# A store moved from GpSimd's DMA queue to ScalarE's, and half of a weight piece asked for two units later, in an mLSTM cell with a SwiGLU block

## The chip, the cores and the metric

The kernel runs on one core of one Trainium2 chip. Its time is device microseconds of one execution; the figure compared is the median of several runs. A core has TensorE (PE), VectorE (DVE), ScalarE (ACT), GpSimd (POOL) and SyncE (SP), each with an instruction stream of its own that it works through in order, and 16 DMA engines that all queues share. SyncE, ScalarE and GpSimd can ask for DMA transfers.

## The reference, cut to what matters

```
# q, k, v, o_gate: (4, 8, 768, 40); i_gate, f_gate: (4, 8, 768); all float32
m = -1e30; C = 0; n = 0
for t in range(768):
    m_new  = max(f_gate[t] + m, i_gate[t])
    f_stab = exp(f_gate[t] + m - m_new); i_stab = exp(i_gate[t] - m_new); m = m_new
    C = f_stab * C + i_stab * outer(v[t], k[t]);  n = f_stab * n + i_stab * k[t]
    y[t] = sigmoid(o_gate[t]) * (C @ q[t]) / max(|n . q[t]|, 1)
x = y as (3072, 320)                      # tokens x (heads * head_dim)
out = (silu(x @ w_gate) * (x @ w_val)) @ w_out     # d_ff = 1536; the weights are float64
```

## The kernel before, in words

The 768 steps are cut into six chunks of 128 tokens. For a chunk the cell is computed in matrix form: scores of q and k, weighted by exponentials of differences of the gates' running sums and running maxima, plus what a state carried from chunk to chunk gives. Each chunk's 512 tokens (four batches) then go through the SwiGLU block. The cell of the next chunk is worked in between the matmuls of the block of the present one. The whole order is written out by hand: every engine gets its instructions in the order of the program text, and semaphores make it wait where data demands it.

The change lies in the block of chunk 0, at some 30 to 95 us. The block's first half runs in twelve units, `hidden(0, m)` for m = 0 to 11 (L741): ten matmuls (20 records in the profile) of x against 128 gate and 128 value columns into two PSUM banks (L749), a SiLU on ScalarE into `tmp` (L754), and a multiply on VectorE into `h_sb` (L755). Behind each unit stand the steps of its slot (`slots`, L1013). They prepare chunk 1: loads, the late gates, transposes, weights.

Meanwhile the weights arrive. They are float64 and are read as pairs of 32-bit words in pieces (`PIECES`, L163). Piece 8 holds blocks 10 and 11, that is gate and value columns of units 10 and 11. `piece_load` (L167) asks for a piece in three parts: part 0, the gate half, on SyncE (640 KB); parts 1 and 2, the value half, on GpSimd (512 and 128 KB). A block is turned into float32 just ahead of use by `convert` (L254): two scalings on ScalarE (`scale`, L227 and L229), a join on VectorE (L236, L237) and an addition (L244) on GpSimd, or for blocks 9 to 11 on VectorE. `ahead` (L1012) says which block is converted inside which unit: block 8 in unit 6, block 9 in unit 7, block 10 in unit 8, block 11 in unit 9. The conversion stands ahead of the unit's SiLU in ScalarE's stream.

The weights of the cell need the running maxima of all later steps in another layout. `late_maxima` (L331) computes them on VectorE into `M_sb`, `M_store` (L343) writes them to `M_dram` in 320 rows of 256 bytes, and `weights_load` (L513) reads them back, spread over partitions, into `w_sb` (two loads of 512 KB). That load is asked for on SyncE and waits for the store's completion. Behind it in SyncE's stream stand the loads of q and v of chunk 1 (`load`, L138), which write rows of 160 bytes, and the gate half of piece 8. `weights_cap` (L529), `weights_sub` (L518) and `weights_exp` (L537) work on `w_sb`. `turn_one` (L347) transposes k in slot 6, and q in the middle of unit 8 (`amid`, L1029); ScalarE copies the results to `kT` and `qT`. The scores (L385) come in slot 8.

The loads and stores asked for by SyncE and ScalarE take eight completion semaphores in turn, those of GpSimd eight others; a transfer waits for the one eight places before it.

Of the kernel before, what the change touches and what calls it, by code (L numbers as in the profile page):

```python
# [13 lines left out]
AF = mybir.ActivationFunctionType  # L14
# [10 lines left out]
def kernel(  # L25
# [18 lines left out]
    nc = tc.nc  # L44
# [63 lines left out]
    k_sb = const.tile([128, BH, DP], F32)  # L108
    q_sb = const.tile([128, BH, DP], F32)
    v_sb = const.tile([128, BH, D1], F32)  # L110
# [3 lines left out]
    kT = const.tile([128, PP, L], F32)  # L114
# [197 lines left out]
    step1 = keep1  # L312
# [250 lines left out]
    A, V, G = nc.scalar, nc.vector, nc.gpsimd  # L563
# [82 lines left out]
    GATE, VALUE = (0,), (1, 2)  # L646
# [357 lines left out]
    def load_all(dst, a, n, eng=nc.sync):  # L1004
# [3 lines left out]
    run = lambda f, *a, **b: (lambda: f(*a, **b))  # L1008
# [4 lines left out]
    slots = {  # L1013
        0: [run(piece_load, 6), run(piece_load, 7, wo_sb)],
        1: [run(late_sums)],
        2: [run(late_maxima), run(M_store, G), run(load_all, k_sb, k, 1)],
        3: [run(late_decay), run(weights_load, 1), run(load_all, q_sb, q, 1), run(load_all, v_sb, v, 1)],
        4: [run(nc.scalar.activation, step1, step1, AF.Exp), run(decay_rows), run(cap_table), run(piece_load, 8)],
        5: [run(late_turns), run(decay)],
        6: [run(turn_one, P, k_sb, kT, (A, A)) for P in range(2)] + [run(weights_cap, 0), run(weights_cap, 1), run(piece_load, 9)],  # L1020
        7: [run(weights_sub, 1, 0), run(weights_sub, 1, 1), run(weights_exp, 0), run(weights_exp, 1), run(weigh_values, G, 0),
            run(weigh_values, G, 1)],
        8: [run(nc.gpsimd.memset, q_sb, 0.0), run(do_scores), run(piece_load, 10), run(load_all, o_sb, o_gate, 1)],
# [128 lines left out]
```

## Time and profile before

| | |
|---|---|
| Time, median of 3 runs | 516.13 us (515.53 to 517.15) |
| Profiled execution: time / span of its instructions | 516.18 us / 514.3 us |
| Mean granted TensorE clock | 0.997 |
| Busy: TensorE, its weight loads | 504.4 us (98%), 425.7 us (83%) |
| Busy: VectorE, ScalarE, GpSimd | 333.0 us (65%), 208.3 us (40%), 264.0 us (51%) |
| Moved by DMA | 43.31 MB in 184187 packets, 173080 of them under 512 B |
| DMA queues, share of 16 engines | SyncE's 45.5%, GpSimd's 4.7% |

A line of a timeline reads: start and length in us, engine, line of the kernel, operation, output <- input, shapes, count, and in brackets how long the engine stood idle before it and what released it. "SPq" is SyncE's queue issuing transfers; such a line lasts as long as the issue, not the transfer. A store or load runs some microseconds on after its issue. Times of single packets and of completions come from the DMA records of the same trace. TensorE's ends are modelled, so a stretch in which it runs at half clock looks busy as well.

### The profile page before, as it was taken

What the parts mean: (1) busy time and instruction counts of PE and PEld (TensorE: products, weight loads), DVE (VectorE), ACT (ScalarE), POOL (GpSimd) and SP (SyncE); (2) the same over time, 40 slices, a digit from 0 to 9 for tenths busy, and PEclk for the clock granted to TensorE, in tenths of its full rate; (3) what the DMA queues carried; (4) which work ended last, traced back from release to release, by engine and by line L of the source; (5) the groups of instructions that cost most, each with busy time, mean ns of one, the idle gap of its engine ahead of it and who ended that gap; (6) DMA issues with size and microseconds to landing.
All of it is one profiled execution on the core that took longest, in us unless ns stands there. A gap on an engine that the chain in (4) does not pass through costs nothing.

```text
span 514.3 us, 15103 instructions
## 1 busy us (share of the span) xinstructions
PE 504.4 (98%) x6437; PEld 425.7 (83%) x6437; DVE 333.0 (65%) x543; ACT 208.3 (40%) x404; POOL 264.0 (51%) x296
## 2 busy tenths in 40 slices
PE   8999989999899999999999999999999999999997
PEld 4854545677788899888899988899988899988897
DVE  5889658697798778578468578558558554233421
ACT  3674846439333339321338321347431330123210
POOL 3674432365689672357652447651447750166710
PEclk9999989999999999999999999999999999999999
DMA  9999997799611992501992411992100200100001
GB/s 147 180 211 229 182 172 213 162 157 108 108 29 26 162 129 39 90 6 25 163 133 35 83 13 20 163 132 40 41 3 16 39 3 20 33 1 0 1 14 40
DMA packets 184187, 43.31 MB, mean 84 GB/s; under 512 B 173080, under 2 KB 179624, under 8 KB 183480
## 3 DMA queue, kind: packets, MB, share of 16 engines
q1 hardware_dynamic: 182308, 36.95, 45.5%
q0 software_dynamic: 1680, 5.33, 4.7%
q8 instruction: 51, 0.84, 0.7%
q14 instruction: 16, 0.13, 0.1%
q10 hardware_dynamic: 132, 0.07, 0.0%
HBM read 35.68 MB, written 4.01 MB: 77 GB/s over the span
## 4 chain that ended last, share of the span: by engine, by line
PE 83%; DMA 7%; ACT 4%; POOL 2%; DVE 1%; SPq 1%; issue 1%; ACTq 0%; POOLq 0%; DVEq 0%
PE gv_x L899 24%; PE o_ps L820 22%; PE gv_y L899 20%; PE gv_ps L749 3%; DMA q_sb<-in_q_dram 3%; PE o_ps L766 3%; DMA raw<-in_moe_w_val_dram 3%; PE inter L434 2%; PE intra L443 2%; PE sp L385 2%; ACT w_sb L535 2%; DMA h_sb<-in_moe_w_val_dram 1%; PE add L411 1%; SPq L369 1%; ACT h_sb L584 1%
## 5 line engine op out<-in xcount | busy, mean ns | idle before, releaser
L899 PE MATMUL gv_x<-xT,wgv_sb 64*128 64x256 f32 x720 | 89.3, 377 | 0.0
L899 PEld LDWEIGHTS gv_x<-xT,wgv_sb 64*128 64x128 f32 x720 | 69.7, 187 | 7.9 <-issue 0.2
L820 PE MATMUL o_ps<-wo_sb,h_sb 128*128 128x160 f32 x480 | 67.4, 300 | 0.0
L820 PEld LDWEIGHTS o_ps<-wo_sb,h_sb 128*128 128x128 f32 x480 | 65.6, 190 | 1.7 <-issue 1.7
L947 ACT ACTIVATE h_sb<-gv_x 128x256 f32<-128x256 f32 x30 | 11.5, 385 | 115.7 <-PE gv_x L899 115.7
L749 PE MATMUL gv_ps<-xT,wgv_sb 64*128 64x512 f32 x240 | 56.2, 612 | 0.1
L749 PEld LDWEIGHTS gv_ps<-xT,wgv_sb 64*128 64x128 f32 x240 | 25.6, 190 | 24.8 <-issue 20.7
L899 PE MATMUL gv_y<-xT,wgv_sb 64*128 64x256 f32 x360 | 44.0, 376 | 0.0
L899 PE MATMUL gv_y<-q_sb,wgv_sb 64*128 64x256 f32 x360 | 44.0, 376 | 0.0
L396 POOL TENSOR_TENSOR vw_sb<-v_sb,w_sb 128x656 f32<-128x656 f32 x10 | 14.0, 1400 | 53.2 <-ACT w_sb L535 40.1
L899 PEld LDWEIGHTS gv_y<-q_sb,wgv_sb 64*128 64x128 f32 x360 | 35.1, 187 | 3.9
L899 PEld LDWEIGHTS gv_y<-xT,wgv_sb 64*128 64x128 f32 x360 | 35.1, 187 | 3.9
L820 PE MATMUL o_ps<-wT,S 128*128 128x160 f32 x240 | 33.4, 299 | 0.0
L820 PEld LDWEIGHTS o_ps<-wT,S 128*128 128x128 f32 x240 | 32.9, 190 | 0.0
L899 PE MATMUL gv_x<-q_sb,sw 64*128 64x256 f32 x240 | 31.1, 377 | 1.4 <-POOL sw L873 1.4
L535 ACT ACTIVATE w_sb<-w_sb,g_T 128x64 f32<-128x64 f32 x128 | 31.0, 335 | 0.0
L920 POOL TENSOR_TENSOR h_sb<-x_sb 128x512 f32<-128x512 f32 x12 | 15.7, 1306 | 24.6 <-ACT x_sb L919 24.6
L940 POOL TENSOR_TENSOR tmp<-tmp 128x512 f32<-128x512 f32 x15 | 20.1, 1342 | 15.0 <-DVE tmp L939 15.0
L920 POOL TENSOR_TENSOR h_sb<-tmp 128x512 f32<-128x512 f32 x13 | 16.5, 1272 | 21.5 <-ACT tmp L919 21.5
L787 POOL TENSOR_TENSOR S<-h_sb 128x256 f32<-128x256 f32 x30 | 22.7, 756 | 9.3 <-DVE h_sb L920 7.3
L899 PE MATMUL gv_y<-q_sb,sw 64*128 64x256 f32 x200 | 27.1, 389 | 0.2 <-DVE tmp L917 0.2
L766 PE MATMUL o_ps<-wo_sb,h_sb 128*128 128x320 f32 x96 | 27.2, 438 | 0.0
(226 smaller groups left out, 988.9 us busy)
## 6 DMA issues: line engine op xcount, KB each, us to landing
w_sb<-M_dram SPq DMA_DIRECT2D x10, 512.0 KB
v_sb<-in_v_dram SPq DMA_DIRECT2D x12, 320.0 KB
o_sb<-in_o_gate_dram SPq DMA_DIRECT2D x12, 320.0 KB
raw<-in_moe_w_out_dram SPq DMA_DIRECT2D x3, 1280.0 KB
k_sb<-in_k_dram SPq DMA_DIRECT2D x10, 320.0 KB
x_sq<-k_sb SPq DMA_DIRECT2D x64, 40.0 KB
q_sb<-in_q_dram SPq DMA_DIRECT2D x32, 64.0 KB
out_dram<-tmp SPq DMA_DIRECT2D x24, 80.0 KB
```

What stands on the lines that cost most here:

```text
L385: nc.tensor.matmul(sp[two][half(i), a, :], lhsT=kT[feats(two), P * UA + a, half(i)], rhs=qT[feats(two), P * UA + a, half(i)], start=True, ...
L396: eng.tensor_tensor(vw_sb[:, heads(P)], v_sb[:, heads(P)], w_sb[:, heads(P), last].to_broadcast([128, UH, D1]), op=ALU.mult)
L434: nc.tensor.matmul(inter[two][half(i), a, :], lhsT=qT[feats(two), P * UA + a, half(i)], rhs=state(2 * n + i)[feats(two), P * UA + a, :], s ...
L535: nc.scalar.activation(w_sb[:, h], w_sb[:, h], AF.Exp, bias=g_T[:, n, h:h + 1], scale=-1.0)
L749: nc.tensor.matmul(ps[i], lhsT=wgv_sb[half(i), m, kc, :], rhs=x[half(i), kc, :], start=(kc == 0), stop=(kc == NKC - 1))
L766: nc.tensor.matmul(ps[u], lhsT=hid(g, m)[:, ts(u, L)], rhs=wo_sb[:, m, :], start=(m == 0), stop=(m == NFC - 1))
L787: eng.tensor_tensor(S1[:, k], lo[:, second_half], hi[:, second_half], op=ALU.add)
L820: nc.tensor.matmul(node[x][:, i], lhsT=lhs(k)[:, ts(i, L)], rhs=rhs(k), start=start and k == 0 and i == 0, stop=stop and k == KH - 1, skip ...
L899: nc.tensor.matmul(ps[:, i, cols], lhsT=lhs(c)[half(i)], rhs=rhs(c)[half(i)], start=start and c == 0, stop=stop and c == n - 1, skip_group ...
L920: (nc.vector if k == KH - 1 else nc.gpsimd).tensor_tensor(h_sb[:, 2 * k + 1], uw[:, 0], uw[:, 1], op=ALU.mult)
L940: nc.gpsimd.tensor_tensor(uw[:, :, second_half], uw[:, :, second_half], uw[:, :, first_half], op=ALU.add)
L947: nc.scalar.activation(h[:, first_half], x[:, 0, first_half], AF.Silu)
```

## The change

The store of the maxima is asked for by ScalarE, at the start of slot 3, where GpSimd asked for it in slot 2. In ScalarE's stream it comes behind the SiLU of unit 3 and ahead of the scalings of block 6; on the other side GpSimd's addition of block 6 no longer has it ahead. Piece 8's gate half stays in slot 4 on SyncE. Its value half moves from slot 4 to the start of slot 6: in GpSimd's stream it comes behind the additions of blocks 7 and 8, where it stood ahead of both. No arithmetic is added or removed. The store takes one of the semaphores that SyncE and ScalarE share, so each later transfer of theirs has the next one.

```diff
-        2: [run(late_maxima), run(M_store, G), run(load_all, k_sb, k, 1)],
-        3: [run(late_decay), run(weights_load, 1), run(load_all, q_sb, q, 1), run(load_all, v_sb, v, 1)],
-        4: [run(nc.scalar.activation, step1, step1, AF.Exp), run(decay_rows), run(cap_table), run(piece_load, 8)],
+        2: [run(late_maxima), run(load_all, k_sb, k, 1)],
+        3: [run(M_store, A), run(late_decay), run(weights_load, 1), run(load_all, q_sb, q, 1), run(load_all, v_sb, v, 1)],
+        4: [run(nc.scalar.activation, step1, step1, AF.Exp), run(decay_rows), run(cap_table), run(piece_load, 8, parts=GATE)],
         5: [run(late_turns), run(decay)],
-        6: [run(turn_one, P, k_sb, kT, (A, A)) for P in range(2)] + [run(weights_cap, 0), run(weights_cap, 1), run(piece_load, 9)],
+        6: [run(piece_load, 8, parts=VALUE)] + [run(turn_one, P, k_sb, kT, (A, A)) for P in range(2)] + [run(weights_cap, 0), run(weights_cap, 1), run(piece_load, 9)],
```

## The prediction

> **What bounds the kernel now.** I read the busy slices first: TensorE is busy for 504.4 us of 514.3, so only what TensorE loses counts. Next, all its waits over 0.15 us behind the first 22 us: 0.40 and 1.57 us at 68 to 70 us, 0.56 at 91.7, 0.37 at 96.2, 1.40 at 137.6, 0.17 at 142.2. The first two are the only ones a load causes, and both are for q of the second chunk (L139). Timeline of TensorE around them (start us, us, line, out<-in, count, wait):
>
> ```profile
> 60.70 7.09 PE L749 MATMUL gv_ps<-xT,wgv_sb 64*128 64x512 f32 x32
> 68.20 0.71 PE L352 MATMUL tp_kq<-x_sq,q_sb 64*128 64x64 f32 x16 [0.40 <-DMA q_sb<-in_q_dram]
> 70.48 0.71 PE L352 MATMUL tp_kq<-x_sq,q_sb 64*128 64x64 f32 x16 [1.57 <-DMA q_sb<-in_q_dram]
> 71.00 3.66 PE L749 MATMUL gv_ps<-xT,wgv_sb 64*128 64x512 f32 x8
> 74.59 2.09 PE L385 MATMUL sp<-qT,kT 40*64 40x64 f32 x128
> ```
>
> Eight matmul records take 3.66 us here, while 40 take 9.76 us later. The table by stretches says why (after each colon: length, busy time by engine, granted clock, DMA share, GB/s):
>
> ```profile
> 54.00:55.40 1.40, 1.40 (x16) 0.99 (x14) 1.26 (x2) 1.38 (x3) 1.26 (x4) 1.00 0.27 30
> 55.40:57.00 1.60, 1.60 (x8) 0.80 (x10) 0.38 (x2) 1.59 (x3) 1.48 (x2) 1.00 1.08 307
> 57.00:62.00 5.00, 5.00 (x52) 2.75 (x50) 3.01 (x7) 3.14 (x7) 1.78 (x2) 1.00 0.98 200
> 67.50:71.10 3.60, 1.63 (x36) 1.25 (x36) 3.53 (x4) 1.09 (x2) 0.00 (x0) 1.00 0.78 120
> 71.10:74.50 3.40, 3.40 (x11) 1.12 (x8) 0.00 (x0) 2.96 (x5) 1.48 (x2) 0.50 1.07 210
> ```
>
> The granted clock is 0.50 for the 3.4 us behind the waits and 1.00 elsewhere after the first microseconds. So this place costs 1.97 us of waiting and 1.7 us of half rate, together 3.7 us. The third thing to see: the DMA engines idle at 54.0 to 55.4.
>
> Why q is late stands in the timelines of SyncE's queue and of GpSimd:
>
> ```profile
> 32.77 18.07 SPq L139 DMA_DIRECT2D k_sb<-in_k_dram  x1
> 53.83 1.18 SPq L516 DMA_DIRECT2D w_sb<-M_dram  x2
> 55.10 8.78 SPq L139 DMA_DIRECT2D q_sb<-in_q_dram  x2
> ...
> 47.06 0.63 POOL L344 DMA_DIRECT2D M_dram<-M_sb  x1 [1.90 <-DVE M_sb L334]
> 54.38 1.17 POOL L202 DMA_DIRECT2D raw<-in_moe_w_val_dram  x2
> ```
>
> and in the list of waits of SyncE's queue (us in total, times, longest):
>
> ```profile
> SPq L516 <- DMA M_dram<-M_sb: 2.9, 1, 2.9
> ```
>
> SyncE is free at 50.84 but waits until 53.83 for the store of the maxima. The store's own packets run only at 51.7 to 53.1, behind the 4 KB packets of earlier value halves on GpSimd's queue. The value half of piece 8 then shares 57 to 62.8 us with the w_sb loads, ahead of q; its gate half is asked for at 70.06.
>
> What comes due next is seen in the timelines of DVE and ACT:
>
> ```profile
> 63.58 2.36 DVE L531 TENSOR_TENSOR w_sb<-w_sb,cap 128x1024 f32<-128x1024 f32 x2 [2.34 <-DMA w_sb<-M_dram]
> 72.03 2.03 ACT L143 COPY qT<-tp_kq 128x512 f32<-128x512 f32 x4
> 77.64 0.80 ACT L227 ACTIVATE top<-raw 128x640 f32<-128x640 f32 x1 [3.59 <-DMA raw<-in_moe_w_gate_dram]
> ```
>
> **Part 1, the store.** GpSimd loses one issue of 0.63 us; its next instruction waits for DVE anyway (48.16), so nothing comes of that. ScalarE gets the issue behind its evacuation of unit 3, which ends at 47.29, and idles then until 49.37. An issue took 0.49 to 0.60 us on SyncE, and 1.14 us on ScalarE at the kernel's start, so it ends by 48.4: nothing on the path. Without that idle time it would be 1.1 us on the conversion of block 6. M_sb is ready at 46.77, before ScalarE comes to it, and the load eight places earlier, whose completion it also waits for, landed long before; queued behind it is that conversion.
>
> When does it land? Unhindered: first packet 1.5 us after the issue (w_sb: 53.83 to 55.40), 0.5 us of packets, 0.8 us from the last packet to the landing (53.02 to 53.81 before), so 50.1. From above: 6.8 us as before, so 54.1. I take 51.5, nearer the first, since the value halves are no longer ahead of it in its queue.
>
> The Trainium skill, "DMA: Bandwidth & Descriptors", "Rules for kernel authors", speaks against this: spreading DMAs over issuing engines gains only issue time, since all run on the same 16 engines. By that alone the store would still land near 53.8 and part 1 would give nothing; the trace shows the 4 KB packets ahead of it, and no run yet a store on ScalarE's queue.
>
> With the store in by 52.5 SyncE asks for w_sb from then on or from 50.84, while k's packets still run (to 54.2, stragglers to 54.9). So w_sb's packets follow at about 54.2, not 55.4: the idle 1.2 us goes.
>
> **Part 2, the value half.** It goes behind the addition of block 8 on GpSimd (59.51 + 1.55 = 61.06). Its first packet came 2.9 us after the issue before, so now at 64.0. GpSimd's next work waits for v and comes at 72, so the issue hides. Earlier, its 1.17 us lay between cap and an addition that waited for DVE until 55.5: nothing gained.
>
> The loads then run thus. The w_sb pair is 1.05 MB: at 307 GB/s (alone, second row of the table) 3.4 us, 4.0 us for the same pair at 106 to 110; it ends at 57.6 to 58.2 and lands by 59.6 instead of 63.46. The q pair is 4096 packets of 160 B; 3136 of them took 3.5 us at 63.5 to 67.0, so 4.6 us: to 62.8. Landing was 1.1 us behind the last packet for 15 engines and 1.4 us more for the sixteenth, which served a 16 KB instruction fetch at 64.3: so q is in at 63.9 to 65.3. TensorE wants the halves at 67.8 and 68.5. Both waits go, with 2 to 4 us to spare, and the half rate behind them.
>
> **What is late next.** TensorE: transposes to 69.2, eight records 1.75 us, to 70.95. The scores need qT, copied behind two exponentials, which need DVE's subtractions. DVE now caps at 61.23 (end of its multiply of unit 6) instead of 63.58. Then the join of block 9, its rounding, and the multiply of unit 7, which waits for ScalarE at 65.85, to 66.5. So the first subtraction starts at 66.5, not 68.68, the exponentials end at 69.95, the first two copies at 70.9. The scores start at 71.0: 3.6 us earlier.
>
> Unit 9 then runs 73.0 to 77.4. Unit 10 needs block 10, whose conversion waits for piece 8's gate half: 77.64 to first matmul 81.10, 3.46 us. Its landing sets the gain. From q's end at 62.8: v 2.8 us (1450 packets a us where it ran freely), the value half 3.3 us (0.66 MB at 200 GB/s), the gate half 3.2 us, 72.1; landing 1.7 us later, 73.8 instead of 77.5: 3.7 earlier, so the scores' 3.6 is the upper end. The lower end is the 1.2 us of idle time that surely goes, if the pauses at 67.5 to 71.1 (DMA share 0.78) come back. I take the middle, 2.4: TensorE waits 1.3 us ahead of unit 10. A wait of 1.40 us at 137.6 brought no half rate.
>
> Later waits hang on conversions, and SyncE's loads from 82.43 on ScalarE's scaling of block 11; they move along. Sum: 516.18 (profiled execution, span 514.3) - 2.4 = 513.8. The median, 516.13, is the same within 0.05.
>
> **Rivals.** (a) *The wait only moves to unit 10.* If the store lands no sooner, or the pauses come back, the gate half comes 1.2 us sooner: 515.0. But TensorE then waits 2.5 us, more than the 1.97 that went ahead of the half rate, and may lose 1.7 us: 516.7. For: ScalarE's 3.59 us wait above. Against: that DMA engines idle where w_sb would fill them.
>
> (b) *The store lands later, and all is slower.* Its 320 rows of 256 B are 20 per DMA engine. If each turn of a 4 KB packet (0.32 us at 48 to 50) let one through, that is 6.8 us from 48.8, landed at 57.0. Then w_sb runs 58.6 to 62.4, q collides with the value half at 64.0 and ends at 70.3, landing 71.4 to 72.8 instead of 70.35. TensorE waits some 2.2 us longer: 518.4. It decides from a landing at about 55 on. Likewise, if ScalarE's issue stuck behind k's descriptors until 50.84, scaling of block 6 would be 1.5 us late. Against: at 48 to 50 us SyncE moved ten 160 B packets for each 4 KB packet, so a turn takes several, and the 4 KB packets end near 51.5.
>
> (c) *The half rate stays.* The only drop follows the wait for q, so I hold the wait to be the cause; if it came at 71 by another cause, eight records take 3.5 us, the scores end at 74.7, unit 9 at 79.1: 2.0 us gained, 514.2. The Trainium skill, "TensorE: Matmul & The Clock Gate", "Part 1", has the half rate after an idle window of some 3.4 us, more than the 1.97 waited here; by that rule this rival would hold, though the 3.4 us of half rate in the trace agree with the page's window.
>
> **How the numbers follow.** Forecast, 512.5 to 514.6: 0.58. (c): 0.05, also faster. (a), 515.0 to 516.7: 0.22, within 0.3% (1.5 us, about what a measurement of this kernel can tell from no change). (b): 0.15, slower. So faster 0.63, same 0.22, slower 0.15. The range runs from 512.5 (gain 3.6) to 516.7 (upper end of (a)) and leaves (b) out.
>
> **What would show it.** Right: the store lands before 52.5; w_sb is asked for near 51 to 52; TensorE does not wait for q; clock 1.00 at 71 to 74.5; scores near 71; ScalarE's scaling of block 10 at 74 to 76.5. Wrong: a wait of 2 us or more ahead of unit 10, w_sb asked for after 53.8, a new stall on ScalarE at 47 to 51, or a gain that is gone by 142 us, from where TensorE has no waits.

## The result: 0.4% slower, with a longer wait ahead of unit 10

The changed kernel takes 518.47 us (median of 19 runs, 515.39 to 520.84), the kernel before 515.85 us (19 runs, 512.38 to 518.99): ratio 1.0043, 95% interval 1.0027 to 1.006. The profiled execution took 519.01 us, its span 517.2 us, mean granted clock 0.993 (before: 516.18, 514.3, 0.997). The mean clock helps in reading single times, since executions differ in how many stretches of 3.41 us at half clock they hold, and one stretch takes about 0.003 off the mean. In the changed kernel 4 of 19 have none (clock 0.998 or more) and average 516.4 us, 8 average 517.5, and 7 at a clock under 0.9945 average 519.4. Ratios below leave out runs more than 1.5% above the fastest of their kernel (one with unit 9 twice, four with all of piece 8 on SyncE).

TensorE's timeline after:

```profile
67.61 0.66 PE L352 MATMUL tp_kq<-x_sq,q_sb 64*128 64x64 f32 x16
68.72 0.71 PE L352 MATMUL tp_kq<-x_sq,q_sb 64*128 64x64 f32 x16 [0.44 <-DMA q_sb<-in_q_dram]
69.24 1.97 PE L749 MATMUL gv_ps<-xT,wgv_sb 64*128 64x512 f32 x8
71.14 2.10 PE L385 MATMUL sp<-qT,kT 40*64 40x64 f32 x128
73.16 4.56 PE L749 MATMUL gv_ps<-xT,wgv_sb 64*128 64x512 f32 x20
83.16 7.27 PE L749 MATMUL gv_ps<-xT,wgv_sb 64*128 64x512 f32 x20 [5.43 <-DVE wgv_sb L244]
90.36 1.14 PE L411 MATMUL add<-vw_sb,k_sb 64*64 64x41 f32 x64
```

The first five lines are what the change was predicted to do: the wait for q is 0.44 instead of 0.40 + 1.57 us, eight records of unit 8 take 1.97 instead of 3.66, and the scores start at 71.14 instead of 74.59, 3.45 us sooner. Then unit 9 ends at 77.72 and TensorE waits 5.44 us for block 10 (in the kernel before unit 10 started at 81.10 with no wait that the profile shows), and unit 10 takes 7.27 us (5.28 before). Its successor L411 starts at 90.36 instead of 86.31: 4.05 us late. Some of that comes back, since the kernel before waits 0.56 and 0.37 us at 91.7 and 96.2 where this one doesn't: 3.2 late at 97, 2.55 at 140. The table by stretches shows the half rate in its new place, and what went before (length, busy time by engine, granted clock, DMA share, GB/s):

```profile
64.00:68.00 4.00, 4.00 (x32) 1.92 (x30) 3.83 (x6) 2.12 (x3) 0.00 (x0) 1.00 1.14 182
70.00:72.00 2.00, 2.00 (x62) 1.09 (x62) 0.00 (x0) 1.89 (x4) 0.00 (x0) 1.00 0.19 23
81.30:88.10 6.80, 4.94 (x11) 3.73 (x13) 6.49 (x10) 4.93 (x7) 0.00 (x0) 0.50 0.40 114
88.10:100.00 11.90, 11.90 (x290) 7.57 (x287) 7.15 (x14) 3.93 (x6) 4.32 (x4) 1.00 0.85 158
```

At 70 to 72 us the DMA engines are nearly idle, although the gate half that unit 10 needs has yet to be loaded. The timelines of SyncE's queue, ScalarE and GpSimd say why:

```profile
32.09 19.44 SPq L139 DMA_DIRECT2D k_sb<-in_k_dram  x2
53.93 1.13 SPq L516 DMA_DIRECT2D w_sb<-M_dram  x2
55.15 5.59 SPq L139 DMA_DIRECT2D q_sb<-in_q_dram  x2
60.84 10.27 SPq L139 DMA_DIRECT2D v_sb<-in_v_dram  x2
71.40 1.10 SPq L202 DMA_DIRECT2D raw<-in_moe_w_gate_dram  x1
...
46.33 0.36 ACTq L344 DMA_DIRECT2D M_dram<-M_sb  x1
...
79.58 0.78 ACT L227 ACTIVATE top<-raw 128x640 f32<-128x640 f32 x1 [7.68 <-DMA raw<-in_moe_w_gate_dram]
...
61.44 1.14 POOL L202 DMA_DIRECT2D raw<-in_moe_w_val_dram  x2
```

SyncE sits in the issue of v for 10.27 us (5.85 before), so the gate half, next in its stream, is asked for at 71.40 (70.06 before) although q went 3 us sooner. In the DMA records all but the last dozen of the value half's 4 KB packets run at 64.4 to 68.1. Meanwhile SyncE's 160 B packets fall from some 860 a us to 14 to 40, and a count shows that these are the last of q's: v, whose issue began at 60.84, sends its first packet at 67.6. The last of the sixteen DMA engines then finishes its share of q, value half, v and gate half 1.0 to 2.8 us behind the other fifteen (0.6 to 1.4 in the kernel before); DMA share drops to 0.19 in that time. The gate half lands at 79.47, where the kernel before had it at 77.54. Fifteen engines are done with it by 78.02, 1.1 us later than before; the last one adds the rest of the 1.9 us.

The store, first line of ScalarE above, was asked for 0.73 us sooner than on GpSimd, and still landed at 53.92 (53.81 before). The chain that ended last, in order of time, holds both loads:

```profile
46.33 7.59 DMA M_dram<-M_sb
...
54.47 6.81 DMA w_sb<-M_dram
...
71.40 8.07 DMA raw<-in_moe_w_gate_dram
```

### The profile page after: what moved, and what is told of

Its sections match the earlier page's. It is cut to its first block, busy times and chain, and to the rows that moved or that the text cites. A ratio compares the mean times of both kernels' runs of the same rounds, so it can differ in the third digit from the quotient of the medians.

```text
span 517.2 us, 15103 instructions
## 1 busy us (share of the span) xinstructions
PE 503.9 (97%) x6437; PEld 425.3 (82%) x6437; DVE 333.1 (64%) x543; ACT 208.0 (40%) x404; POOL 264.0 (51%) x295
## 4 chain that ended last, share of the span: by engine, by line
PE 83%; DMA 5%; ACT 4%; DVE 4%; POOL 2%; SPq 1%; issue 1%; DVEq 0%; ACTq 0%; POOLq 0%
PE gv_x L899 24%; PE o_ps L820 22%; PE gv_y L899 20%; PE gv_ps L749 4%; PE o_ps L766 3%; PE inter L434 2%; PE intra L443 2%; DMA raw<-in_moe_w_gate_dram 2%; ACT w_sb L535 1%; DMA M_dram<-M_sb 1%; DMA w_sb<-M_dram 1%; PE add L411 1%; PE sp L385 1%; SPq L369 1%; ACT h_sb L584 1%
## 5 line engine op out<-in xcount | busy, mean ns | idle before, releaser
L749 PE MATMUL gv_ps<-xT,wgv_sb 64*128 64x512 f32 x240 | 56.5, 618 | 5.5 <-DVE wgv_sb L244 5.4
L396 POOL TENSOR_TENSOR vw_sb<-v_sb,w_sb 128x656 f32<-128x656 f32 x10 | 14.0, 1398 | 53.8 <-ACT w_sb L535 40.2
## 6 DMA issues: line engine op xcount, KB each, us to landing
w_sb<-M_dram SPq DMA_DIRECT2D x10, 512.0 KB
```

The source lines that it names most:

```text
L396: eng.tensor_tensor(vw_sb[:, heads(P)], v_sb[:, heads(P)], w_sb[:, heads(P), last].to_broadcast([128, UH, D1]), op=ALU.mult)
L749: nc.tensor.matmul(ps[i], lhsT=wgv_sb[half(i), m, kc, :], rhs=x[half(i), kc, :], start=(kc == 0), stop=(kc == NKC - 1))
```

## Experiments

The theory from the two traces: the store's move gives nothing; the value half, asked for later, stands in v's way instead of that of w_sb and q; v's issue holds up the gate half; and unit 10 pays. The rivals are a cost from the store or from ScalarE's issue, and a half rate that comes by itself. Lines in diffs are cut to the items that move.

**The store alone**, in the kernel before.

```diff
-        2: [run(late_maxima), run(M_store, G), ...
+        2: [run(late_maxima), ...
-        3: [run(late_decay), run(weights_load, 1), ...
+        3: [run(M_store, A), run(late_decay), run(weights_load, 1), ...
```

> Only the store moves to ScalarE; the value half stays in slot 4. Theory A (the value half, asked for at 61.4 us, holds the DMA engines at 64 to 68 us and so makes v and the gate half of piece 8 late; the store lands no sooner, since its packets come behind those of the k loads): the store lands at 53 to 54.5 us, TensorE waits some 2 us for q as before, 515.9 us within 0.8 of the kernel before. Theory B (the store on ScalarE does the harm, by what it does to SyncE's loads): 517.5 or more. The prediction's part 1 (store in by 52.5): 514.9 or less.

Measured: 516.32 us, ratio 1.0003 (0.999 to 1.0016). The store lands at 53.2, w_sb is asked for at 53.20, and q still comes late:

```profile
67.82 0.71 PE L352 MATMUL tp_kq<-x_sq,q_sb 64*128 64x64 f32 x16 [0.42 <-DMA q_sb<-in_q_dram]
69.85 0.71 PE L352 MATMUL tp_kq<-x_sq,q_sb 64*128 64x64 f32 x16 [1.31 <-DMA q_sb<-in_q_dram]
70.37 1.96 PE L749 MATMUL gv_ps<-xT,wgv_sb 64*128 64x512 f32 x8
...
80.22 4.13 PE L749 MATMUL gv_ps<-xT,wgv_sb 64*128 64x512 f32 x16 [1.37 <-ACT tmp L754]
```

The last line matters most. This execution had no half rate behind q, so the scores came at 72.26, 2.3 us sooner than before, and TensorE waited 1.37 us ahead of unit 10 instead: ScalarE's scalings of block 10 stand ahead of the SiLU (L754) that it waits for, and the gate half was in at 76.7. So in this execution more than half of the 2.3 us was lost again ahead of unit 10, which started at 80.22 instead of 81.10.

**The value half alone**, in the kernel before.

```diff
-        4: [..., run(piece_load, 8)],
+        4: [..., run(piece_load, 8, parts=GATE)],
-        6: [run(turn_one, ...
+        6: [run(piece_load, 8, parts=VALUE)] + [run(turn_one, ...
```

> Only the value half moves to slot 6; the store stays on GpSimd in slot 2. Theory A: like the changed kernel, 517.5 to 519.5 us; scores near 71 us, gate half in at 78.5 to 79.5, TensorE waits 4 to 6 us ahead of unit 10 and runs at half rate behind it. Theory B: 513 to 514.5, no wait above 2 us ahead of unit 10.

Measured: 517.99 us, 1.0036 (1.002 to 1.0052); the half rate lies at 82.41 to 89.24. SyncE's issue of v, and TensorE's unit 10:

```profile
61.00 10.11 SPq L139 DMA_DIRECT2D v_sb<-in_v_dram  x2
...
83.45 7.78 PE L749 MATMUL gv_ps<-xT,wgv_sb 64*128 64x512 f32 x20 [5.67 <-ACT tmp L754]
```

The whole loss is this part's.

**Why the store doesn't land sooner.** In the changed kernel k's loads go behind the load of w_sb, so that SyncE has nothing in issue when ScalarE asks for the store.

```diff
-        2: [run(late_maxima), run(load_all, k_sb, k, 1)],
+        2: [run(late_maxima)],
-        3: [run(M_store, A), run(late_decay), run(weights_load, 1), run(load_all, q_sb, q, 1), ...
+        3: [run(M_store, A), run(late_decay), run(weights_load, 1), run(load_all, k_sb, k, 1), run(load_all, q_sb, q, 1), ...
```

> The changed kernel, but SyncE asks for k of chunk 1 behind the loads of w_sb, so that no long issue of SyncE is under way when ScalarE asks for the store at 46 to 47 us. Theory G (the store's packets come late because they are made behind those of k): its packets run at 47.5 to 49.5 and it lands by 51. Rival H (ScalarE's queue itself gets few turns against the other two): it lands at 53 or later as in the changed kernel. Its time says little, since k comes late: 515 to 520.

Measured, one run: 517.41 us; timelines of ScalarE and SyncE:

```profile
46.44 0.37 ACTq L344 DMA_DIRECT2D M_dram<-M_sb  x1
...
51.08 1.12 SPq L516 DMA_DIRECT2D w_sb<-M_dram  x2
52.31 5.45 SPq L139 DMA_DIRECT2D k_sb<-in_k_dram  x2
```

Packets at 48.6 to 50.6 instead of 51.7 to 53, landing at 51.06: 4.6 us after the issue, where it was 7.6. Here they run beside the value halves' 4 KB packets, the last of which ends at 50.34, so those alone don't hold the store. In the changed kernel it sends its first packet at 51.72, just behind the end of SyncE's issue of k (51.53), and then runs beside k's packets. In all five kernels with the store on ScalarE and k in its place, the first packet came 0.2 to 0.8 us behind the end of that issue. So it stood behind k's issue, not behind GpSimd's queue. (k is then late, and TensorE waits 1.44 and 1.77 us for it, so this is no improvement.)

**The gate half ahead of v**, in the changed kernel.

```diff
-        3: [..., run(load_all, q_sb, q, 1), run(load_all, v_sb, v, 1)],
+        3: [..., run(load_all, q_sb, q, 1), run(piece_load, 8, parts=GATE), run(load_all, v_sb, v, 1)],
-        4: [..., run(piece_load, 8, parts=GATE)],
+        4: [...],
```

> The changed kernel, but SyncE asks for piece 8's gate half between q and v of chunk 1 instead of behind v. Theory A: the gate half lands at 70 to 73 us, the wait ahead of unit 10 falls under 1 us, no half rate, scores near 71: 512 to 513.5 us. Rival C (something else, such as the landing of the value half itself or ScalarE's and VectorE's conversion chain, would hold unit 10 anyway): 516 or more, with unit 10 still starting after 81 us.

Measured: 515.42 us, ratio to the kernel before 0.9996 (0.9973 to 1.0018). The gate half is in at 74.87 (on fifteen engines by 72.06, the last 2.8 us behind), where 70 to 73 was expected; v's issue takes 10.45 us without holding it up, the profiled execution has no half rate, and unit 10 starts at 80.30. One of the twelve runs took 521.98. The loss is gone; the gain of 3 to 4 us isn't there. Timelines of GpSimd, VectorE and TensorE:

```profile
76.32 1.30 POOL L396 TENSOR_TENSOR vw_sb<-v_sb,w_sb 128x656 f32<-128x656 f32 x1 [14.35 <-DMA v_sb<-in_v_dram]
77.99 1.48 POOL L396 TENSOR_TENSOR vw_sb<-v_sb,w_sb 128x656 f32<-128x656 f32 x1 [0.36 <-DMA v_sb<-in_v_dram]
...
76.33 1.98 DVE L237 SCALAR_TENSOR_TENSOR wgv_sb<-top,wgv_sb 128x640 uint32<-128x640 uint32 x1
78.44 1.71 DVE L244 CUSTOM_DVE_ANT_0 wgv_sb<-wgv_sb,low 128x1280 uint16<-128x1280 uint16 x1
...
80.30 5.07 PE L749 MATMUL gv_ps<-xT,wgv_sb 64*128 64x512 f32 x20 [2.15 <-DVE wgv_sb L244]
```

VectorE's second and third step of block 10 take 1.98 and 1.71 us (0.83 each before), just where GpSimd multiplies v, which now lands late: that is 2.0 us of the missing time.

**Unit 9 twice**, in the changed kernel: ten more matmuls, so that TensorE has work while it waits for block 10. The second pass starts the sums anew, so it only takes time.

```diff
-        for kc in range(NKC):
+        for kc in [c for n in range(2 if m == 9 else 1) for c in range(NKC)]:
```

> The changed kernel with the ten matmuls of unit 9 issued twice (the second pass starts its sums anew, so the result is the same): 4.36 us more work for TensorE just ahead of the wait for block 10. Theory A with the half rate as a consequence of that wait: the extra work lies inside the wait, the wait shrinks to about 1 us, the granted clock stays 1.00, and the time falls by 2 to 3.4 us against the changed kernel, to 515 to 516.5, though work was added. Rival D (the half rate has another cause, or the wait is not what it looks like): no faster than the changed kernel, 518 or more.

Measured: 517.86 us, 1.0034 (1.0009 to 1.0059). The profiled execution had 4.3 us more work and no half rate, and was 1.5 us faster than the changed kernel's:

```profile
73.87 8.85 PE L749 MATMUL gv_ps<-xT,wgv_sb 64*128 64x512 f32 x40
83.50 5.28 PE L749 MATMUL gv_ps<-xT,wgv_sb 64*128 64x512 f32 x20 [0.77 <-ACT tmp L754]
```

Unit 10 starts at 83.50, later by about the 0.33 us by which SyncE asked for the gate half later, and takes 5.28 instead of 7.27 us: in this execution the matmuls put into the wait are free, and with the wait filled there is no half rate. A clock of 0.998 or more came in 7 of 12 runs (changed kernel: 4 of 19); the median shows no clear gain, and the 515 to 516.5 expected were missed.

**Two other places for the value half**, in the kernel before: slot 3 (gate half left in slot 4), and slot 5.

```diff
+        3: [run(piece_load, 8, parts=VALUE), ...          (first kernel)
+        5: [run(piece_load, 8, parts=VALUE), ...          (second kernel)
```

> The kernel before, but piece 8's value half is asked for in slot 3, one unit earlier than before instead of two later; store on GpSimd, gate half in place. Theory A (all that stands ahead of the gate half in the DMA engines sets its landing, and the engines idle at 54 to 55.4 us): the value half's packets start near 53 to 54, fill that idle time, q is in by 66 to 67.5, TensorE waits for it under 0.7 us, scores at 71 to 72.5, gate half in at 74.5 to 76.5: 514 to 515.3 us. Rival E (it only delays k of chunk 1 and w_sb by as much): TensorE waits at the transposes of k at 59.7, 516 or more.

> The value half in slot 5, between the two kernels; store on GpSimd. Theory A: its first packet comes near 60 us, in the middle of w_sb's second half and q; q lands at 67 to 70 and TensorE may wait for it up to 1.5 us; the gate half lands at 77 to 79.5; 516 to 518.5 us, between the two kernels. The prediction's reading (what is out of the way of w_sb pays): 514 to 515.

Measured: slot 3, 518.57 us, 1.0045 (1.0026 to 1.0064); slot 5, 516.13 us, 1.0004 (0.999 to 1.0019). In slot 3, where 514 to 515.3 was expected, the packets run at 52 to 56.5 amid k's, and TensorE waits for both k and q (the profiled execution, 516.69, is the shortest of the eleven); in slot 5 they run at 62 to 65.4 ahead of q's second half. First kernel's TensorE, then the second's:

```profile
62.32 0.71 PE L352 MATMUL tp_kq<-x_sq,k_sb 64*128 64x64 f32 x16 [1.71 <-DMA k_sb<-in_k_dram]
71.56 0.71 PE L352 MATMUL tp_kq<-x_sq,q_sb 64*128 64x64 f32 x16 [1.12 <-DMA q_sb<-in_q_dram]
75.82 0.32 PE L385 MATMUL sp<-qT,kT 40*64 40x64 f32 x2 [1.77 <-ACT qT L143]
```

```profile
70.36 0.71 PE L352 MATMUL tp_kq<-x_sq,q_sb 64*128 64x64 f32 x16 [2.19 <-DMA q_sb<-in_q_dram]
80.62 5.28 PE L749 MATMUL gv_ps<-xT,wgv_sb 64*128 64x512 f32 x20 [1.26 <-ACT tmp L754]
```

Wherever the value half goes, the load of small rows beside it pays, k, q or v in turn.

**All of piece 8 on SyncE, between q and v**, in the kernel before: one queue, in the order of need.

```diff
-                eng = nc.gpsimd if x or 1 < p < 6 else nc.sync
+                eng = nc.gpsimd if (x and p != 8) or 1 < p < 6 else nc.sync
-        3: [..., run(load_all, q_sb, q, 1), run(load_all, v_sb, v, 1)],
-        4: [..., run(piece_load, 8)],
+        3: [..., run(load_all, q_sb, q, 1), run(piece_load, 8), run(load_all, v_sb, v, 1)],
+        4: [...],
```

> The kernel before, but all of piece 8 is asked for by SyncE, between q and v of chunk 1, so that gate half and value half stand in one queue in the order of their use and nothing of GpSimd's queue is in the way. Theory A: q in at 63.5 to 66, both halves in by 71 to 74, the wait ahead of unit 10 under 1 us, clock 1.00, scores near 71: 512.5 to 514 us. Rival F (v, now last, lands at 76 to 78 and holds GpSimd's products and the additions at 83 to 86): 515.5 or more.

Measured: 518.71 us median of all twelve runs, but spread from 513.13 to 522.69; ratio, without the four longest, 1.001 (0.9981 to 1.004). Four runs at a clock of 0.998 or more take 513.1 to 515.0, the other eight 518.1 to 522.7. In the profiled one, of 514.03, unit 10 starts at 77.83, 3.3 us sooner than before, and then the steps of block 11 on VectorE are slow:

```profile
78.79 1.80 POOL L1008 MEMSET q_sb<- 128x2048 f32 x1
...
78.20 2.73 DVE L236 TENSOR_SCALAR wgv_sb<-top 128x640 uint32<-128x640 uint32 x1
80.97 1.23 DVE L237 SCALAR_TENSOR_TENSOR wgv_sb<-top,wgv_sb 128x640 uint32<-128x640 uint32 x1
...
84.82 0.28 PE L411 MATMUL add<-vw_sb,k_sb 64*64 64x41 f32 x2 [1.93 <-DVE w_sb L392]
```

VectorE's first step takes 2.73 us (0.49 before); it starts just ahead of GpSimd's zeroing and ends 0.3 us behind it. TensorE then waits 1.93 us for the weights of the scores (L392), which VectorE makes behind these steps.

**GpSimd's work out of VectorE's way.** The previous kernel (all of piece 8 on SyncE), with the zeroing and the decayed states ahead of the products of v.

```diff
-        7: [..., run(weigh_values, G, 0), run(weigh_values, G, 1)],
-        8: [run(nc.gpsimd.memset, q_sb, 0.0), run(do_scores), ...
-        9: [run(do_weigh, 0), run(do_weigh, 1), run(do_decayed, 2)],
+        7: [...],
+        8: [run(nc.gpsimd.memset, q_sb, 0.0), run(do_decayed, 2), run(weigh_values, G, 0), run(weigh_values, G, 1), run(do_scores), ...
+        9: [run(do_weigh, 0), run(do_weigh, 1)],
```

> Edit: the kernel before with piece 8 asked for by SyncE between q and v (f3_piece8_on_sync), and GpSimd's zeroing of q_sb and its two decayed states put ahead of its two products of v, into the time in which it waits for v. In f3 DVE's three steps of block 11 took 2.73, 1.23 and 1.14 us beside this work, where the kernel before has 0.49, 0.82 and 0.83, and TensorE waited 1.93 and 0.32 us for DVE's weights at 84.8 and 85.4 us. Theory J (GpSimd's work slows DVE beside it, and nothing else holds TensorE there): the zeroing starts near 69 us, the first step of block 11 takes under 1 us, the wait at 84.8 goes to under 0.3; the span falls from f3's 512.3 to 510.3 and the time to 512.0 in an execution without half rate. Theory H (the half rate comes behind TensorE's waits of 1 to 2 us): with no wait of 1 us left before 135 us, the spread of f3 (513.1 to 522.7) is mostly gone and the median is 512 to 513.5, 0.992 to 0.995 of the kernel before. Rival K (the half rate comes whatever the waits): the best runs are near 512, but the median stays at 515 to 518.

Measured: 513.62 us (513.02 to 515.22, 5 runs), ratio 0.9946 (0.9933 to 0.9959): faster than both kernels. All five runs have a clock of 0.998 or more, where the previous kernel had this in four of twelve; that fits a half rate that follows TensorE's waits. Its TensorE, and GpSimd's zeroing in its new place:

```profile
73.12 2.13 PE L385 MATMUL sp<-qT,kT 40*64 40x64 f32 x126 [0.16 <-ACT qT L143]
75.18 9.24 PE L749 MATMUL gv_ps<-xT,wgv_sb 64*128 64x512 f32 x40
84.52 0.28 PE L411 MATMUL add<-vw_sb,k_sb 64*64 64x41 f32 x2
...
70.92 1.80 POOL L1008 MEMSET q_sb<- 128x2048 f32 x1 [8.10 <-PE tp_kq L352]
```

Units 9 and 10 run without a gap and the 1.93 us wait is gone, as expected; the time is 1.6 us above the 512.0 hoped for. In the profiled execution (515.22, the longest of the five) everything is already 2.4 us later at 60 us than in the kernel it was made from, with a wait of 0.94 us at 43.2 for the conversion of a block, far ahead of the edit; of the step that should take under 1 us, 1.62 is left, beside the second product.

**The same for the gate half ahead of v.** The kernel with the gate half ahead of v, the same move, and block 10's rounding on GpSimd ahead of the products.

```diff
-    ahead = {..., 8: [10], ...}
+    ahead = {..., 8: [], ...}
+        first += {8: [run(scale, 10), run(join, 10)], ...
+        8: [run(nc.gpsimd.memset, q_sb, 0.0), run(do_decayed, 2), run(rounded, 10), run(weigh_values, G, 0), run(weigh_values, G, 1), ...
```

> Edit: e3_gate_ahead_of_v with the zeroing and the decayed states ahead of the products as in h1, and with block 10's rounding on GpSimd, in order ahead of the products. In e3 DVE's second and third step of block 10 took 1.98 and 1.71 us beside the products (0.83 each in the kernel before), and unit 10 began at 80.30 behind a wait of 2.15. Theory J: the second step takes 0.83, GpSimd's rounding 1.56, unit 10 begins at 78.7 to 79.1 behind a wait of 0.6 to 1.0; the products then lie beside DVE's steps of block 11, which cost under 1 us on TensorE. Time 514.0 to 514.6 in an execution without half rate, median 514 to 515.5. Rival (block 10's conversion was slow because the gate half's last rows came late, not because of GpSimd): the second step still takes over 1.5 us, and unit 10 begins at 80 or later: median as e3, 515.4.

Measured: 515.62 us, 0.9989 (0.9974 to 1.0004), no clear gain. The mechanism held: the second step is back at 0.83 us, unit 10 starts at 79.16 behind 0.68 us. But block 11's steps took the blow (1.37 and 1.81 us) and TensorE waits 0.89 us at 84.9.

**The move of GpSimd's work alone**, in the kernel before (same lines as two above, loads untouched).

> Edit: the kernel before with only GpSimd's zeroing and decayed states ahead of its products of v. In the kernel before TensorE has no wait behind these steps, and the loads stand as they were. Theory J expects no change: 516.0, ratio 0.998 to 1.002. Rival (the order of GpSimd's work is worth something by itself, so that h1's gain says nothing of the loads): 514.5 or less.

Measured: 516.37 us, 1.0012 (0.9995 to 1.0028): no difference shown, so the gain needs the order of the loads.

## Why the prediction was wrong, step by step

**Part 1, the store: wrong.** Hidden on ScalarE, yes (an issue of 0.36 us at 46.33). Landing at 51.5, no: 53.92, inside the range given (50.1 to 54.1), at its bad end. The working took the 4 KB packets on GpSimd's queue for the obstacle; the run with k behind shows it was SyncE's issue of k. So w_sb was asked for at 53.93, not before 52.5. The Trainium skill's "DMA: Bandwidth & Descriptors", "Rules for kernel authors", by which a change of issuing engine gains only issue time, gave the right sum here: 516.32 us with the store alone.

**Part 2, q and the scores: right in the main.** First packet 64.4 (64.0 predicted); scores at 71.14 (71.0); clock 1.00 at 71 to 74.5. w_sb in at 61.3 rather than 59.6, since part 1 failed; q's halves in at 63.6 and 65.8 (63.9 to 65.3), with the last engine at 68.6, which left 0.44 us of the waits. The prediction took that last engine to be the one that served an instruction fetch; the records don't say which engine it was. How much of the wait stays varies: the other kernels with q's loads as in the changed one and the value half in slot 6 waited 0.65 (value half alone), 1.80 (unit 9 twice), 0.27 and 1.39 us (gate half ahead of v, two kernels). The value half alone is what moved this.

**"Its landing sets the gain ... I take the middle, 2.4": the step that failed.** The chain was right, and its terms were mis-sized. From q's end the sum had v 2.8, value half 3.3, gate half 3.2 us, one behind the other, each at a rate read elsewhere in the kernel before. In fact the value half's packets took 3.7 us, for most of which v sent none while SyncE could not go on; then came a pause while one engine finished behind the others. v's issue, by kernel:

| value half's packets beside v | v's issue, us |
|---|---|
| no: before, store alone, GpSimd's work moved alone, slot 3, piece 8 on SyncE (two kernels) | 5.85, 5.61, 5.16, 4.92, 7.09 and 6.48 |
| yes: changed, value half alone, unit 9 twice, gate half ahead of v (two kernels), k behind | 10.27, 10.11, 10.89, 10.45 and 10.29, 8.93 |
| in part: slot 5 | 8.90 |

Instead of 73.8 the gate half landed at 79.47. Of these 5.7 us, 1.8 are q's, whose packets, bar the last few, ended at 64.55 and not 62.8, since part 1 failed. 2.8 are v's and the value half's, 8.9 us for 6.1. 1.8 are the gate half's, 5.0 us for 3.2: all but its last twenty packets took 3.3, the rest ran on to 78.46. The landing behind the last packet took 0.7 less. The bound "the 1.2 us of idle time that surely goes" was no lower end either: that gain was the store's, which didn't come, and a loss was never in the range of this term.

**"Together 3.7 us" at the old place: only partly to be had.** In the kernel before, the 1.7 us of half rate were in part hidden behind block 10. Its executions with a clock of 0.998 or more are only 0.3, 0.9 and 1.2 us faster on average than the others (in sets of 36, 28 and 23 runs), and the store alone shows the wait that takes its place. The prediction did bound the gain by the moment when block 10 would be there; it was that moment that it had wrong.

**Rivals.** (a), the wait moving to unit 10 and the half rate with it, is what happened, but with the gate half 1.9 us later where (a) had it 1.2 sooner: the wait was 5.44 us instead of 2.5, and unit 10 took 2.0 us longer than before (7.27 against 5.28) instead of 1.7, so 518.5 and not 516.7. (b) named nearly the measured time by luck: the store was no later. (Its own sum, 48.8 + 6.8 + 0.8, comes to 56.4 and not 57.0; and its ten small packets for each of 4 KB are an average of two unlike stretches, 54 to 47 at 48 to 49 us and 564 to 16 at 49 to 50.) (c) fell: at 71 to 74.5 the clock was 1.00, and in the profiled executions the half rate moved with the wait; the two runs that filled or shortened the wait (unit 9 twice, gate half ahead of v) had none. Among "what would show it wrong", three of four came: the wait of 2 us or more ahead of unit 10, w_sb asked for after 53.8, and a gain gone by 142 us.

## What to carry to other kernels

Moving a transfer out of the way of one load puts it in the way of the next: cost the whole queue up to the next operand that is needed, with what each load does beside the other and not alone. A stall's price is bounded by when the next operand arrives. And of two loads in one stream, ask first for the one that TensorE needs first; here all of piece 8 ahead of v, with GpSimd's work kept away from VectorE's conversion, made 0.5%.

## What the runs showed of the hardware

- A store asked for by ScalarE ran no packet while SyncE's issue of k was still under way: packets 5.4 us after the issue, and 2.1 us where SyncE had nothing in issue.
- While a transfer in 4 KB packets from GpSimd's queue ran, SyncE's loads of 160 B rows fell from some 860 packets a us to 14 to 40, the rest of q's, and v's load, in issue since 60.84, sent no packet until 67.6.
- One DMA engine of sixteen ended 1.0 to 2.8 us behind the rest in the changed kernel, and 0.6 to 1.4 in the kernel before. A 16 KB instruction fetch of 1.58 us at 62.1 us ran on one engine; whether on this one, and whether it is the cause, was not tried.
- VectorE and GpSimd slow each other: VectorE's steps of 0.49 and 0.83 us took 2.73 and 1.98 beside GpSimd's zeroing and products, and GpSimd's decayed states 2.24 instead of 1.43. The Trainium skill, "SBUF — State Buffer", "SBUF: two separate sides", has some of VectorE's instructions share a port pair with GpSimd's, which one instruction holds to its end while the other is blocked. The step of 2.73 us fits: it began amid a product (77.31 to 78.84), had the zeroing right behind that, and ended 0.3 us after the zeroing.
- The half clock comes in pieces of 3.41 us (3.41 before, 6.83 after), and waits of the same size bring it in one execution and not in the next: 0.40 + 1.57 us did in the kernel before and 1.44 + 1.77 us with k behind; 1.80 (unit 9 twice), 2.19 (value half in slot 5) and 2.15 (gate half ahead of v) did not in the profiled executions. The Trainium skill, "TensorE: Matmul & The Clock Gate", "Part 1", has a free-running window of that length. The 5.44 us wait contains a whole one (77.88 to 81.29, ahead of the drop); the 1.97 us in the kernel before are less than one, so a whole idle window is not needed in every case.
